# The last block's output stores: one transfer for each batch's 64 rows in place of one for two batches

## Chip, cores and metric

The kernel runs on one core of one Trainium2 chip. The metric is the device time of one execution in microseconds. Before the change it is 1684.03 us, the median of three runs (1682.93 to 1684.46).

## What is computed

A linear attention without softmax, normalized by its root mean square, then two feed-forward layers over the 4608 tokens (8 batches of 576):

```python
kv  = einsum('bhsd,bhse->bhde', k, v)          # q, k, v: (8, 8, 576, 64)
o   = einsum('bhsd,bhde->bhse', q, kv)
o   = o / sqrt(mean(o * o, -1) + 1e-6) * g_norm
x   = o.transpose(0, 2, 1, 3).reshape(4608, 512)
r   = maximum(x @ w_in1, 0)                    # w_in1: (512, 2048)
x   = (s * r * r + b) @ w_out1                 # w_out1: (2048, 512)
h   = x @ w_in2
out = (h / (1 + exp(-h))) @ w_out2             # out: (4608, 512)
```

## The kernel before

Every matmul operand is split into a rounded high part and the rest, and a product is three matmuls of 128 x 512 (`mm3`, lines 182 to 185). Tokens are taken in nine blocks of 512 columns (`NB`, `T`). Blocks 0 to 7 are the first 512 tokens of each batch. The ninth, called the last block here, gathers the 64 tokens that each of the eight batches has left (`REM` = 64, and 8 x 64 = 512).

Layer 1 takes the nine blocks one after the other (`unit`, lines 596 to 707) and writes its result to a scratch tensor in DRAM. Layer 2 takes blocks 0 to 7 in four pairs, by a scheme with seven products in place of eight (`hidden` and `outputs`, lines 820 to 954), and the last block by `unit` again, mixed with the last pair. Both kinds end in a tile with tokens on the 128 partitions and 512 output features in each row.

The order of the work is set by a planner (`Plan`, lines 16 to 116). Each operation has a key, the engines it may run on with a cost on each, and what it needs; the planner plays this through and issues the instructions in the order that comes out. All ordinary transfers are issued by SyncE (SP) through the helper `dma` in line 200, so all of them stand in the profile as L200.

What matters here runs at the very end. `block_out` (lines 709 to 736) takes a finished accumulator `a_t[d]` of the last block: `out_y` copies it to a part of the tile `x_t` (line 723, helper line 195; ScalarE does all four of them here), and `store` sends it to `out` (lines 731 and 732). There are four such accumulators, d = 0 to 3, one for each 128 of the block's 512 tokens, so that partitions 0 to 63 hold the last tokens of batch 2d and partitions 64 to 127 those of batch 2d + 1. In the tensor `out` the 64 rows of one batch lie in one piece, and those of the next batch lie 576 rows further on. `n = P // REM` is 2.

Between the second and the third of these four stores, the last pair's outputs are finished: VectorE adds the last products to a tile `y` (`total`, line 940), and SyncE stores it, 128 rows in one piece (line 953). Five such stores stand between them. The planner costs a store of `block_out` at 0.48 us on SyncE and 0.73 us of transfer (line 736).

Of the kernel before, what the change touches and what calls it, by code (L numbers as in the profile page):

```python
# [15 lines left out]
class Plan:  # L16
# [19 lines left out]
    def add(self, engines, key, fn, needs=(), makes=(), takes=(), gives=(), move=None, opens=(), until=None):  # L36
        self.ops.append((key, len(self.ops), engines, fn, needs, makes, takes, gives, move, opens, until))
        for b in gives:
            self.users[b] = self.users.get(b, 0) + 1
# [80 lines left out]
def kernel(  # L120
# [22 lines left out]
    B, H, S, D = q.shape  # L143
    NT, DM = out.shape
    DFF = w_in1.shape[1]
    P = 128
# [4 lines left out]
    T = NCH * P  # L151
    REM = S - T
# [40 lines left out]
    def copy(e, dst, src):  # L193
        if e == "ACT":
            nc.scalar.copy(dst, src)
        else:
            eng[e].tensor_copy(dst, src)

    def dma(dst, src):
        nc.sync.dma_start(out=dst, in_=src)  # L200
# [167 lines left out]
    def new_x(t):  # L368
        x_t[t] = xp.tile([P, KD, T], F32, tag="x32", name="x32")
# [339 lines left out]
    def block_out(layer, t, d, key, acc):  # L709
        lb = layer * NB + t  # L710
        st = {}
        yb = ("y", (lb, d))

        final = lb == 2 * NB - 1

        def out_y(e):
            if not final:
                st["y"] = tp.tile([P, T], F32, tag="y", name="y", bufs=2)
            else:
                if d == 0:  # L720
                    new_x(lb + 1)
                st["y"] = x_t[lb + 1][:, d]
            copy(e, st["y"], a_t[d])

        def store(e):
            if layer == 0:
                dma(y1[t, :, d], st["y"])
            elif t < NB - 1:
                dma(out[t * S + d * P:t * S + (d + 1) * P, :], st["y"])
            else:  # L730
                n = P // REM
                dma(out.rearrange("(b s) e -> b s e", s=S)[n * d:n * (d + 1), T:, :], st["y"])

        add({ACT: 0.52, DVE: 0.6}, key, out_y, needs=[("mm2", lb * KF + KF - 1, d)], makes=[("yc", lb, d)],
            takes=[("x32", lb + 1)] * (d == 0) if final else [yb], gives=[acc])
        add({"SP": 0.48}, key + 0.1, store, needs=[("yc", lb, d)], makes=[("y", lb, d)], gives=[] if final else [yb], move=0.73)
# [354 lines left out]
```

## Time and profile before

| | |
|---|---|
| median of three runs | 1684.03 us (1682.93 to 1684.46) |
| time of the profiled execution | 1683.55 us |
| its span | 1681.2 us |
| TensorE busy with matmuls | 1642.5 us, 98% of the span |
| VectorE, ScalarE, GpSimd busy | 51%, 39%, 34% |
| transfers | 236.28 MB, 141 GB/s in the mean |
| mean granted TensorE clock | 0.991 |

The span goes from the first instruction of the profiled execution to its last one; its own time is 2.35 us longer. Times in the views are counted from the start of the span. A share of busy DMA engines is that of all 16 together, so that one engine that works all the time is 0.0625. "To landing" is the time from the start of a transfer's issue to its completion, and the time in a row of an issue is how long SyncE was held by it. `out_dram<-x` are the four stores of the last block, `out_dram<-y` those of the pairs.

### The profile page before, as it was taken

To read this page: it belongs to the slowest core of one execution; us is meant where nothing else is said; L and a number is where in the kernel's file an instruction comes from. 1 tells how busy PE (TensorE), PEld (TensorE's weight loads), DVE (VectorE), ACT (ScalarE), POOL (GpSimd) and SP (SyncE) were. 2 spreads that over 40 slices of the span, in tenths; PEclk is the share of its full clock that TensorE was granted. 3 is DMA by queue.
4 is the path that set the end of the run, shared out by engine and by line. 5 is a ranking of instruction groups with operands and counts; after the bars stand their busy time and mean duration, and the time that the engine had idled before them with its cause. 6 is when DMAs were issued, how large, how long until landed. Compare 5 with 4: busy or idle time off the path is not lost.

```text
span 1681.2 us, 21306 instructions
## 1 busy us (share of the span) xinstructions
PE 1642.5 (98%) x7744; PEld 1334.1 (79%) x7744; DVE 865.4 (51%) x1313; ACT 658.5 (39%) x1198; POOL 565.3 (34%) x481
## 2 busy tenths in 40 slices
PE   8889999999999999999999999999999999999995
PEld 6667888888888888888887888888888888888884
DVE  6998666675656666534342244634463445344211
ACT  5666444444444444432333322432343234323221
POOL 4665343333434344210341223622362235223100
PEclk9989999999999999999999999999999999999998
DMA  9554445444444544210134444644464447444552
GB/s 218 173 157 125 134 127 158 139 147 126 138 143 129 168 122 150 99 63 1 51 116 128 126 145 140 229 156 143 142 232 148 139 138 237 138 140 141 183 156 81
DMA packets 226911, 236.28 MB, mean 141 GB/s; under 512 B 99832, under 2 KB 181752, under 8 KB 226680
## 3 DMA queue, kind: packets, MB, share of 16 engines
q1 hardware_dynamic: 226680, 234.94, 45.4%
q8 instruction: 61, 1.00, 0.3%
q14 instruction: 42, 0.34, 0.1%
q0 software_dynamic: 128, 0.00, 0.0%
HBM read 181.41 MB, written 53.48 MB: 140 GB/s over the span
## 4 chain that ended last, share of the span: by engine, by line
PE 91%; DVE 3%; DMA 1%; ACT 1%; issue 1%; SPq 1%; POOL 0%; DVEq 0%; ACTq 0%; POOLq 0%
PE hp L836 18%; PE h L184 8%; PE h L185 8%; PE h L183 8%; PE acc L183 8%; PE acc L184 7%; PE acc L185 7%; PE acc L931 7%; PE acc L932 7%; PE acc L930 7%; PE kv_ps L433 1%; PE acc L687 1%; PE acc L686 1%; PE acc L685 1%; DVE raw L263 1%
## 5 line engine op out<-in xcount | busy, mean ns | idle before, releaser
L836 PE MATMUL hp<-xo,win 128*128 128x512 f32 x1344 | 344.0, 390 | 0.8 <-DVE tmp L861 0.8
L191 POOL TENSOR_TENSOR g<-tmp,g 128x512 fp32r<-128x512 f32 x123 | 159.3, 1296 | 425.0 <-ACT g L188 223.5
L836 PEld LDWEIGHTS hp<-xo,win 128*128 128x128 f32 x1344 | 252.0, 188 | 57.6 <-DVE tmp L861 2.2
L940 DVE TENSOR_TENSOR y<-acc,y 128x512 f32<-128x512 f32 x224 | 154.3, 690 | 275.1 <-PE acc L932 273.0
L183 PE MATMUL acc<-gh,wo 128*128 128x512 f32 x576 | 234.4, 407 | 2.9 <-ACT gh L188 2.9
L184 PE MATMUL acc<-gl,wo 128*128 128x512 f32 x576 | 226.9, 394 | 5.8 <-DVE gl L191 2.8
L629 ACT ACTIVATE g<-h 128x512 f32<-128x512 f32 x160 | 95.5, 597 | 346.8 <-PE h L185 337.6
L184 PE MATMUL h<-xl,wi 128*128 128x512 f32 x576 | 226.8, 394 | 1.7 <-DVE xl L191 1.6
L183 PE MATMUL h<-xh,wi 128*128 128x512 f32 x576 | 226.5, 393 | 0.1
L185 PE MATMUL h<-xh,wi 128*128 128x512 f32 x576 | 226.1, 393 | 0.3 <-DVE wi L191 0.3
L185 PE MATMUL acc<-gh,wo 128*128 128x512 f32 x576 | 226.1, 392 | 0.0
L637 DVE SCALAR_TENSOR_TENSOR g<-g,vecs 128x512 f32<-128x512 f32 x128 | 104.0, 813 | 197.1 <-ACT g L629 197.0
L932 PE MATMUL acc<-wout,g 128*128 128x512 f32 x512 | 201.7, 394 | 0.0
L931 PE MATMUL acc<-wout,g 128*128 128x512 f32 x512 | 201.7, 394 | 0.0
L930 PE MATMUL acc<-wout,g 128*128 128x512 f32 x512 | 201.3, 393 | 0.0
L861 DVE TENSOR_TENSOR tmp<-hp,tmp 128x512 f32<-128x512 f32 x160 | 110.4, 691 | 99.3 <-PE hp L836 93.9
L665 DVE SCALAR_TENSOR_TENSOR gl<-g,vecs,gh 128x512 fp32r<-128x512 f32 x128 | 112.4, 878 | 49.3 <-ACT gh L659 48.1
L282 POOL TENSOR_TENSOR dw<-raw 128x256 uint32<-128x256 uint32 (+1 forms) x100 | 88.8, 890 | 137.3 <-DVE raw L268 87.3
L184 PEld LDWEIGHTS acc<-gl,wo 128*128 128x128 f32 x576 | 108.9, 189 | 28.1 <-DVE gl L191 4.4
L191 POOL TENSOR_TENSOR spill<-dw,spill 128x512 fp32r<-128x512 f32 x53 | 71.5, 1350 | 176.5 <-ACT spill L188 171.2
L184 PEld LDWEIGHTS h<-xl,wi 128*128 128x128 f32 x576 | 109.0, 189 | 27.2 <-DVE xl L191 3.7
L183 PEld LDWEIGHTS acc<-gh,wo 128*128 128x128 f32 x576 | 109.0, 189 | 26.4 <-ACT gh L188 4.2
(123 smaller groups left out, 2303.1 us busy)
## 6 DMA issues: line engine op xcount, KB each, us to landing
win<-wi SPq DMA_DIRECT2D x96, 512.0 KB, 4.5
wout<-wo SPq DMA_DIRECT2D x160, 256.0 KB, 4.1
wi<-spill SPq DMA_DIRECT2D x32, 512.0 KB, 2.6
wo<-spill SPq DMA_DIRECT2D x32, 512.0 KB, 2.9
win<-wi SPq DMA_DIRECT2D x64, 256.0 KB, 3.2
raw<-in_moe_w_out_dram SPq DMA_DIRECT2D x38, 256.0 KB, 3.0
y<-y SPq DMA_DIRECT2D x36, 256.0 KB, 2.6
raw<-in_moe_w_in_dram SPq DMA_DIRECT2D x34, 256.0 KB, 2.8
```

Source lines behind the costliest of these rows:

```text
L183: nc.tensor.matmul(ps, wh, xh, start=first, stop=False)
L184: nc.tensor.matmul(ps, wh, xl, start=False, stop=False)
L185: nc.tensor.matmul(ps, wl, xh, start=False, stop=last)
L191: eng[e].tensor_tensor(lo, src, f32(hi), op=ALU.subtract)
L637: nc.vector.scalar_tensor_tensor(out=g_t[u], in0=g_t[u], scalar=s_t, in1=g_t[u], op0=ALU.mult, op1=ALU.mult)
L665: nc.vector.scalar_tensor_tensor(out=st["g"][1], in0=g_t[u], scalar=b_t, in1=f32(st["g"][0]), op0=ALU.add, op1=ALU.subtract)
L836: nc.tensor.matmul(ps, w[:, wn, f_], x_[:, xn], start=first and n == 0, stop=kk == KH - 1 and n == 2, skip_group_check=True)
L861: nc.vector.tensor_tensor(t, bank[me, a], tmp[b_, me], op=ALU.add)
L930: nc.tensor.matmul(ps, g[:, 0, dd], w[:, 0], start=f == 0, stop=False)
L931: nc.tensor.matmul(ps, g[:, 0, dd], w[:, 1], start=False, stop=False)
L932: nc.tensor.matmul(ps, g[:, 1, dd], w[:, 0], start=False, stop=f == 1)
L940: nc.vector.tensor_tensor(y2[tp, tt], st["ps"], y2[tp, tt], op=ALU.add)
```

## The change

In the last block's branch of `store`, a loop over the two batches takes the place of the one transfer. Each transfer reads 64 partitions of the tile and writes 64 whole rows of `out`, which lie in one piece. Bytes and destinations are the same; four transfers of 256 KB become eight of 128 KB.

```diff
             elif t < NB - 1:
                 dma(out[t * S + d * P:t * S + (d + 1) * P, :], st["y"])
             else:
-                n = P // REM
-                dma(out.rearrange("(b s) e -> b s e", s=S)[n * d:n * (d + 1), T:, :], st["y"])
+
+                for i in range(P // REM):
+                    r = (P // REM * d + i) * S + T
+                    dma(out[r:r + REM, :], st["y"][i * REM:(i + 1) * REM])
```

The planner's costs for the operation are as before. On SyncE's queue, this is what stands at the end of the program before the change: the last load of weights, two stores of the last block (`x`, in the form 2 x 64 x 512), the five stores of the last pair (`y`), and the other two of the last block. Names in square brackets are what an instruction waits for; `DMAHW0` to `DMAHW7` are the eight semaphores that transfers take in turn, and a wait on one of them is for the transfer that had it before.

```order
L200 DMA wout<-wo_7_98 128x2x256
L200 DMA out_dram<-x_13837 2x64x512 [waits Activation_49] x2
L200 DMA out_dram<-y_12251 128x512 [waits DMAHW4_49,DVE_49]
L200 DMA out_dram<-y_12269 128x512 [waits DMAHW5_49,DVE_49]
L200 DMA out_dram<-y_12285 128x512 [waits DMAHW6_49,DVE_49]
L200 DMA out_dram<-y_12307 128x512 [waits DMAHW7_49,DVE_49]
L200 DMA out_dram<-y_12330 128x512 [waits DMAHW0_49,DVE_49]
L200 DMA out_dram<-x_13837 2x64x512 [waits DMAHW1_49,Activation_49]
L200 DMA out_dram<-x_13837 2x64x512 [waits DMAHW2_49,Activation_49]
```

The same place in the changed kernel, on SyncE, from the second store of the last block on (two more halves, those of the first store, stand just ahead):

```order
L200 DMA out_dram<-x_13837 64x512 [waits DMAHW4_49,Activation_49]
L200 DMA out_dram<-x_13837 64x512 [waits DMAHW5_49]
L200 DMA out_dram<-y_12251 128x512 [waits DMAHW6_49,DVE_49]
L200 DMA out_dram<-y_12269 128x512 [waits DMAHW7_49,DVE_49]
L200 DMA out_dram<-y_12285 128x512 [waits DMAHW0_49,DVE_49]
L200 DMA out_dram<-y_12307 128x512 [waits DMAHW1_49,DVE_49]
L200 DMA out_dram<-y_12330 128x512 [waits DMAHW2_49,DVE_49]
L200 DMA out_dram<-x_13837 64x512 [waits DMAHW3_49,Activation_49]
L200 DMA out_dram<-x_13837 64x512 [waits DMAHW4_49]
L200 DMA out_dram<-x_13837 64x512 [waits DMAHW5_49,Activation_49]
L200 DMA out_dram<-x_13837 64x512 [waits DMAHW6_49]
```

Each store of the last block has become two in the same place, and nothing has moved past another; the semaphore that a store takes has shifted by two for the y stores and by two to four for the last ones. The other engines have the same instructions in the same order.

## Rows read from the trace of the kernel before

**Rows 1.** Chain of waits, its last pieces: start us, us, what.

```profile
1662.01 0.24 PE acc L687
...
1662.28 0.59 ACT x L195
```

**Rows 2.** Busy time by stretches of the program's end, columns as in the first line.

```profile
core 0: us, PE busy (x) PEld busy (x) DVE busy (x) ACT busy (x) POOL busy (x), PEclk, DMA share, GB/s
1647.50:1654.50 7.00, 7.00 (x33) 5.77 (x32) 0.69 (x1) 2.37 (x4) 0.00 (x0) 1.00 0.00 0
1654.50:1658.00 3.50, 3.50 (x17) 2.84 (x16) 1.38 (x2) 0.04 (x1) 0.00 (x0) 1.00 0.13 33
1659.00:1662.00 3.00, 3.00 (x15) 2.30 (x13) 1.38 (x2) 0.40 (x1) 0.00 (x0) 1.00 0.94 287
1662.00:1664.00 2.00, 0.24 (x2) 0.00 (x0) 0.00 (x0) 0.77 (x2) 0.00 (x0) 1.00 0.85 244
1665.00:1680.00 15.00, 0.00 (x0) 0.00 (x0) 0.00 (x0) 0.00 (x0) 0.00 (x0) 0.51 0.13 49
1680.00:1681.20 1.20, 0.00 (x0) 0.00 (x0) 0.00 (x0) 0.00 (x0) 0.00 (x0) 0.50 0.00 0
```

**Rows 3.** SyncE's waits after 1663 us: total us, times, longest us.

```profile
SPq L1086 <- DMA out_dram<-x: 13.0, 2, 7.9
```

**Rows 4.** Timeline of SyncE's issues at the end: start us, us, what.

```profile
1653.26 0.65 SPq L200 DMA_DIRECT2D out_dram<-x  x1
...
1656.06 2.15 SPq L200 DMA_DIRECT2D out_dram<-y  x1
1658.31 0.45 SPq L200 DMA_DIRECT2D out_dram<-y  x1
1658.85 0.87 SPq L200 DMA_DIRECT2D out_dram<-y  x1
...
1661.64 0.33 SPq L200 DMA_DIRECT2D out_dram<-y  x1
1662.21 0.52 SPq L200 DMA_DIRECT2D out_dram<-x  x1
1662.89 4.05 SPq L200 DMA_DIRECT2D out_dram<-x  x1
```

**Rows 5.** Line 200, the y stores issued at 1656.06 and at 1661.64.

```profile
DMA to landing us min/median/max: 11.0/11.0/11.0
...
DMA to landing us min/median/max: 8.0/8.0/8.0
```

**Rows 6.** Transfers by line, 353 to 361 us: count, KB each, median us to landing.

```profile
y<-y SPq DMA_DIRECT2D x4, 256.0 KB, 2.5
```

**Rows 7.** Timeline of SyncE's issues, 350.9 to 354.4 us.

```profile
350.96 0.61 SPq L200 DMA_DIRECT2D rem<-in_k_dram  x1
351.61 0.60 SPq L200 DMA_DIRECT2D rem<-in_v_dram  x1
354.35 0.34 SPq L200 DMA_DIRECT2D y<-y  x1
```

**Rows 8.** Busy time by stretches, 353.0 to 353.6 us, columns as in rows 2.

```profile
353.00:353.20 0.20, 0.20 (x2) 0.17 (x1) 0.20 (x1) 0.00 (x0) 0.17 (x1) 1.00 0.25 58
353.20:353.40 0.20, 0.20 (x2) 0.16 (x2) 0.20 (x1) 0.00 (x0) 0.00 (x0) 1.00 0.33 73
353.40:353.60 0.20, 0.20 (x3) 0.15 (x2) 0.20 (x1) 0.00 (x0) 0.00 (x0) 1.00 0.37 80
```

**Rows 9.** Timeline of ScalarE, 1661 to 1663 us.

```profile
1661.60 1.26 ACT L195 COPY x<-acc 128x512 f32<-128x512 f32 x2 [7.06 <-PE acc L687]
```

**Rows 10.** SyncE's issues on the tile orem_d, 32 stores of 32 KB.

```profile
DMA to landing us min/median/max: 1.4/1.8/4.8
```

## Prediction

> **What bounds the kernel now.** I read the views from the end of the program backwards, since the edited line runs only there. The chain of waits comes first, and the reader should see where it stops: after the last matmul at 1662.01 us it takes one ScalarE copy at 1662.28 and ends at 1662.87, 18.3 us before the span is over at 1681.2 [rows 1]. The chain follows work on engines; what fills those 18.3 us has to be read from the transfers.
>
> The table by stretches shows it [rows 2]. From 1659 to 1662 the 16 DMA engines were busy for 0.94 of the time and moved 287 GB/s. From 1665 to 1680 they were busy for 0.13 and moved 49 GB/s, with every compute engine at zero. A share of 0.125 is two engines of sixteen at work all the time, 24.5 GB/s each. The same 0.13 stands in 1654.5 to 1658, when the first two stores of the last block were the only transfers in flight (nothing moved from 1647.5 to 1654.5). SyncE's waits agree: at the program's end it waits 13.0 us in two pieces for out_dram<-x, the stores of the last block [rows 3]; counted from the end of its last issue (1662.89 + 4.05 = 1666.94 us [rows 4]) that puts the last landing at 1679.94, and 1.2 us of closing steps follow.
>
> The reason lies in the form of the store. It is 2 batches x 64 rows x 512, and the share says that it is divided over its outermost count, two. Four such stores are 1.05 MB; the five stores in 128 x 512 form among them spread over all engines and give the same two engines another 2/16 of 1.31 MB, 0.16 MB. 1.21 MB at 49 GB/s is 24.7 us; from 1654.5 (first bytes) to 1679.9 are 25.4 us, so this queue on two engines, begun by the first of the four stores, explains the whole tail. Its traces are also in the other stores: the y store issued at 1656.06 held SyncE for 2.15 us [rows 4] and took 11.0 us to land, and that of 1661.64, when the other fourteen engines were nearly free, still 8.0 [rows 5]; the same 128 x 512 form took 2.5 us in the middle of the program [rows 6]. So **two DMA engines bound the last 18 us**; TensorE bounds the rest and is not touched.
>
> **The change, part by part.**
>
> *Spread.* Each 2 x 64 x 512 store becomes two of 64 x 512, whose outermost count is 64 rows on both sides. I take them to run on all sixteen engines, as the 128 x 512 stores do. The trace has one kind with 64 rows, the loads of the remainder rows: issued at 350.96 and 351.61, with no other issue until 354.35, they are what is left in flight at 353.0 to 353.6, at a share of 0.25 to 0.37, four to six engines [rows 7, 8]. So 64 rows spread over more than two. In a sentence by itself: the Trainium skill, page "DMA: Bandwidth & Descriptors", section "Why a DMA increments its semaphore by 16 and not by 1", gives as the number of engines the largest one up to 16 that divides the slowest sizes of both sides, which is two before (this trace agrees, 0.13) and sixteen after (no run shows that yet).
>
> *Four more issues on SyncE.* The two extra ones at 1653 to 1655 lie in its idle time. The other two lie on the path. The third store is released at 1662.21 as now, the fourth by the copy that ends at 1662.86 [rows 4, 9]. I price an issue by the unhindered 128 x 512 store, 0.33 us, plus 0.09 to the next instruction (0.45 from 1658.31 leaves 0.09 before 1658.85) [rows 4]: halves at 1662.21, 1662.63, 1663.05, and the last at 1663.47. Bounds: nothing extra (the last at 1662.89), or the 0.61 and 0.60 of the 64-row loads [rows 7], with which the last begins 0.84 us later, 1664.3.
>
> *Waits added.* The order gives the stores eight semaphores in turn, so that four more stores reach round sooner: the last y store waits for a half of the first store, and the last four for halves of the first two and for the first y store. All of those are issued by 1656.1 and would land some 3 us later, while the waits stand at 1661.6 and after. I cost them at nothing; that holds as long as the early halves land within 5 us. Nothing is queued behind the last of them but the end of the program.
>
> *The last landing.* From issue to landing a 256 KB store took 2.5 us [rows 6], a 32 KB one 1.8 in the median and at least 1.4 [rows 10]. For the last 128 KB half I take 2.4, close to the larger one, since three halves are just ahead of it: 1663.47 + 2.4 = 1665.9. The rate gives a check: first bytes come about 1.25 us after an issue (1653.26 to 1654.5), so those of the last y store at 1662.9; it and the last two blocks are 0.79 MB, at 287 GB/s 2.7 us, hence 1665.6. The lower bound is 1663.47 + 1.4 = 1664.9.
>
> *What stays.* TensorE, ScalarE, VectorE and GpSimd keep their order, and no instruction on them waits for these stores. The 1.2 us of closing steps stay.
>
> **The sum.** The end moves from 1681.2 to 1665.9 + 1.2 = 1667.1, a gain of 14.1 us. Against the profiled execution's own 1683.55 us that is 1669.45. The median of the runs shown, 1684.03, stands 0.48 above that execution, so for the median I forecast **1669.9 us**. With the lower landing it is 1.0 less, 1668.9. What bounds the end then is TensorE's last matmul, one copy, the last store and the closing steps.
>
> **A rule that speaks against it.** The rows show that one 2 x 64 x 512 store in two batches runs on two engines [rows 2]. The Trainium skill's page "DMA: Bandwidth & Descriptors", section "Rules for kernel authors", advises not to split a transfer into its two partition halves, because both halves use the same sixteen engines and go one after the other. By that rule alone two issues of 0.42 us would be added and nothing gained, 1684.9. The premise of sixteen engines isn't met by the store of this kernel, by the 0.13 of the row, so I give it only the weight of the third rival below.
>
> **The rivals.**
>
> 1. *Half the rate for half the partitions.* Each new store reads only rows 0 to 63 or 64 to 127 of its tile. If half the partitions yield half the rate, the last 0.52 MB go at 144 GB/s instead of 287: 3.65 us in place of 1.83, the end 1.8 us later, **1671.7**. For it: no row shows a large transfer from 64 partitions on many engines. Against: halves of both kinds follow each other and could overlap. The Trainium skill, page "SBUF — State Buffer", section "Door 1: The DMA port swizzle (why [64,N] ≈ [32,N])", says that 64 partitions reach eight of sixteen ports; no row here tests it. Chance 0.20.
>
> 2. *One engine (slower).* If the engines followed the number of batches in a store, one batch would have one engine: the same one for all eight halves. It would carry 1.05 MB plus 1/16 of 1.31 MB, 1.13 MB at 24.5 GB/s, 46.1 us from 1654.5, to 1700.6, plus 1.2: the span grows by 20.6, the median to **1704.6**. It decides for fewer than two engines; at two the time stands still. For it: two batches had exactly two. Against: the loads of 64 rows at a share of 0.25 to 0.37, where one engine is 0.06 [rows 8]. Chance 0.03.
>
> 3. *No change.* If the two engines come from something that stays (the tile, the output's rows), the same bytes drain in the same time, 1684.0, at most 0.9 more for two later issues. Against: the y stores go to the same output tensor at a share of 0.94 among others [rows 2]. Chance 0.02.
>
> **How the numbers follow.** My forecast has 0.75. Of the cases, forecast and half rate are faster: 0.95; no change 0.02; slower 0.03. A measurement of this kernel can tell about 0.2% from no change, 3.4 us, and both faster cases are well beyond it. The range takes in the lower landing (1668.9) less the 1.0 us or so by which the quickest run shown stands under the median, and above, half rate with the slow issues, 1671.7 + 0.8: **1667.9 to 1672.5**.
>
> **What would show it.** In the changed kernel's table by stretches no stretch at 0.13 is left in the tail; the share from 1655 to 1662 lies between 0.4 and 0.7, moves in bursts, and falls to zero by about 1666. The y store at 1656.06 no longer holds SyncE for 2 us, and all y stores land in about 2.5 to 3 us. SyncE's wait for out_dram<-x shrinks from 13.0 to about 2, and the span is near 1667. Half rate would show in the last halves: the share at 1663 to 1666 near 0.5 and a later end. I am wrong if a stretch of 0.06 or 0.13 remains, if the issues on SyncE are longer than 0.6 us each, or if one of the added waits stands before 1661.6 on a half that hasn't landed.

## Result, and the profile after

The changed kernel takes 1669.3 us in the median of four runs (1667.89 to 1669.53), the kernel before beside it 1683.62 (1682.93 to 1684.46): a ratio of 0.9913, with a 95% interval of 0.9896 to 0.993, or 14.3 us. The forecast was 1669.9, with a range of 1667.9 to 1672.5. The profiled execution took 1669.53 us with a span of 1667.3.

The stretches of the program's end, in the changed kernel, columns as in [rows 2]:

```profile
1654.50:1658.00 3.50, 3.50 (x17) 2.84 (x16) 1.38 (x2) 0.00 (x0) 0.00 (x0) 1.00 0.85 216
1655.00:1662.00 7.00, 7.00 (x31) 5.46 (x30) 3.46 (x5) 0.49 (x1) 0.00 (x0) 1.00 0.66 207
1664.00:1666.00 2.00, 0.00 (x0) 0.00 (x0) 0.00 (x0) 0.00 (x0) 0.00 (x0) 1.00 0.84 184
```

No stretch at 0.13 is left. Where two engines began to work off the first store alone at 33 GB/s [rows 2], 216 GB/s move now, and everything has landed by 1666.3.

SyncE's waits from 1650 us on, in the changed kernel (total us, times, longest us), answer to [rows 3]:

```profile
SPq L200 <- ACT x L195: 8.8, 2, 8.6
SPq L200 <- DVE y L942: 4.1, 5, 1.0
SPq L1088 <- DMA out_dram<-x: 1.5, 3, 0.6
```

The wait for the landings at the program's end fell from 13.0 to 1.5 us. There is no row in which L200, an issue, waits for a transfer: the semaphores' waits cost nothing. SyncE's issues, in the changed kernel, answer to [rows 4]:

```profile
1653.17 0.54 SPq L200 DMA_DIRECT2D out_dram<-x  x1
...
1655.97 0.36 SPq L200 DMA_DIRECT2D out_dram<-y  x1
...
1662.12 0.47 SPq L200 DMA_DIRECT2D out_dram<-x  x1
1662.64 0.59 SPq L200 DMA_DIRECT2D out_dram<-x  x1
1663.33 0.55 SPq L200 DMA_DIRECT2D out_dram<-x  x1
1663.92 0.59 SPq L200 DMA_DIRECT2D out_dram<-x  x1
```

No issue is held for 2 or 4 us any more. Of the ten stores issued from 1655 us on (the five y stores, the second store's second half and the last four halves), from issue to landing:

```profile
DMA to landing us min/median/max: 2.0/2.2/2.5
```

The first of the y stores takes 2.1 us and the last 2.0, where [rows 5] had 11.0 and 8.0; each of the last four halves takes 2.3 to 2.4, and the last landing is at 1666.3.

The last matmul of the changed kernel begins here, and is 0.39 us long:

```profile
1661.76 0.39 PE L687 MATMUL acc<-wout,gl 128*128 128x512 f32 x1
```

So it ends at 1662.15, and **the tail behind it**, from there to the end of the span, is 5.1 us (the span before rounding is 1667.25). Before it was 18.9 (1681.17 less 1662.24: the last matmul began at 1661.85). The difference, 13.8 us, is nearly the whole gain; TensorE's part did not change. The tail is the measure of choice for what follows, since the end of the last matmul itself varies: it is 1662.15 and 1663.21 us in two profiles of the changed kernel, and lies between 1661.8 and 1665.2 in the twelve profiles of this study. Work far ahead of these stores varies by more than a microsecond.

### The profile page after: what moved, and what is told of

Read it like the earlier page. It is cut to its first block, busy times and chain, and to the rows that moved or that the text cites. A ratio compares the mean times of both kernels' runs of the same rounds, so it can differ in the third digit from the quotient of the medians.

```text
span 1667.3 us, 21311 instructions
## 1 busy us (share of the span) xinstructions
PE 1641.2 (98%) x7744; PEld 1334.0 (80%) x7744; DVE 866.3 (52%) x1313; ACT 658.2 (39%) x1198; POOL 564.8 (34%) x481
## 4 chain that ended last, share of the span: by engine, by line
PE 91%; DVE 4%; DMA 1%; issue 1%; SPq 1%; ACT 1%; POOL 0%; DVEq 0%; ACTq 0%; POOLq 0%
PE hp L838 18%; PE h L184 8%; PE h L185 8%; PE h L183 8%; PE acc L183 8%; PE acc L184 7%; PE acc L185 7%; PE acc L933 7%; PE acc L934 7%; PE acc L932 7%; PE kv_ps L433 1%; DVE raw L263 1%; SPq L200 1%; PE acc L685 1%; PE acc L686 1%
```

## Experiments

The theory: the outermost count of a store's form sets how many DMA engines carry it, two before and sixteen now, and those two were a queue that began with the first store. The rivals: smaller transfers as such; the last stores alone; half the rate for half the partitions; one engine for one batch.

**More transfers without more engines.**

```diff
-                for i in range(P // REM):
-                    r = (P // REM * d + i) * S + T
-                    dma(out[r:r + REM, :], st["y"][i * REM:(i + 1) * REM])
+                n = P // REM
+                for c in range(2):
+                    cc = slice(c * DM // 2, (c + 1) * DM // 2)
+                    dma(out.rearrange("(b s) e -> b s e", s=S)[n * d:n * (d + 1), T:, cc], st["y"][:, cc])
```

> Each of the four stores is cut into two by columns, so that there are eight of 128 KB as in the change, but each still has two batches as its outermost count. My theory (the outermost count sets the engines): two engines carry the same 1.21 MB, the tail stays at a DMA share of 0.13 from 1665 us to the end, and the time is that of the kernel before, 1684, or up to 3 us more, since the pieces are half as long. Rival (smaller and more transfers are what helps): about 1669 to 1672.

Measured: 1684.62 us (1683.99 to 1686.1), a ratio of 1.0007 to the kernel before (0.9997 to 1.0018). A stretch of its end:

```profile
1668.00:1681.00 13.00, 0.00 (x0) 0.00 (x0) 0.00 (x0) 0.00 (x0) 0.00 (x0) 0.50 0.13 46
```

Eight transfers of 128 KB, as in the change, and the share stays at two of sixteen engines. The number and size of the transfers give nothing here, as long as the outermost count stays two.

**The split on the last two stores alone, and on the first two alone.** The loop stays, with the old transfer ahead of it for two of the four; in the second run the condition is `d >= 2`:

```diff
+                if d < 2:
+                    n = P // REM
+                    dma(out.rearrange("(b s) e -> b s e", s=S)[n * d:n * (d + 1), T:, :], st["y"])
+                    return
                 for i in range(P // REM):
```

> Only the third and the fourth store are split by batch, the first two stay as before. My theory (a queue on two engines): these two carry 0.52 MB of the first two stores and 2/16 of 1.84 MB, 0.75 MB at 49 GB/s, 15.4 us from 1654.5, so the last landing is at 1669.9, the span 1671 and the time 1673.2, 11 us under the kernel before. Rival (only the form of the last stores counts, the early ones are hidden behind matmuls): 1669.3, the full gain.

> Only the first and the second store are split by batch, the last two stay as before. My theory: the two engines begin with the third store, first bytes at 1663.4, and carry 0.52 MB at 49 GB/s, 10.7 us, so the last landing is at 1674.1, the span 1675 and the time 1677.4. Rival (the queue that the first store begins is what makes the tail): 1669 to 1671.

Measured: with the last two split 1674.62 us (1673.99 to 1675.4), a ratio of 0.9946 (0.993 to 0.9963); with the first two split 1679.96 (1677.65 to 1681.31), 0.9975 (0.9965 to 0.9984). Both rivals fall, as neither pair alone gives the full gain. Both medians lie above the theory's numbers, by 1.4 and 2.6 us.

In the first run, one issue waits for a transfer (SyncE's waits from 1663 us on):

```profile
SPq L200 <- DMA out_dram<-x: 2.8, 1, 2.8
```

By the rotation of the eight semaphores that is a half of the fourth store, issued only at 1666.13, when the second store, still on two engines, has landed. This is the added wait that the prediction priced at nothing under the condition that the early halves land early; here they don't. But it isn't shown to cost anything. The first half of the third store, issued at 1661.93 without such a wait, takes 7.7 us to land (1669.6), and the last half of all, issued at 1666.72, takes 3.9 (1670.6). Stretches of this run:

```profile
1655.00:1658.00 3.00, 3.00 (x15) 2.42 (x14) 1.53 (x3) 0.00 (x0) 0.00 (x0) 1.00 0.13 35
1667.00:1669.00 2.00, 0.00 (x0) 0.00 (x0) 0.00 (x0) 0.00 (x0) 0.00 (x0) 0.50 0.65 165
1669.40:1669.90 0.50, 0.00 (x0) 0.00 (x0) 0.00 (x0) 0.00 (x0) 0.00 (x0) 0.50 0.13 49
```

The fourth store's halves move mostly between 1667 and 1669; what comes last is two engines alone, at 0.13, which work off their queue. The profiled execution (1673.99) is 0.8 us over the theory's 1673.2, and the first row gives about that much: for 3.0 us the queue moved 35 GB/s where the theory took 49, which is 0.04 MB, 0.9 us at 49 GB/s. The median is another 0.6 us over this execution.

In the second run the tail is one long stretch on two engines, after an early part at full width:

```profile
1655.00:1658.00 3.00, 3.00 (x15) 2.42 (x14) 1.38 (x2) 0.00 (x0) 0.00 (x0) 1.00 0.93 239
1663.50:1667.00 3.50, 0.00 (x0) 0.00 (x0) 0.00 (x0) 0.00 (x0) 0.00 (x0) 0.63 0.12 31
1667.00:1675.00 8.00, 0.00 (x0) 0.00 (x0) 0.00 (x0) 0.00 (x0) 0.00 (x0) 0.50 0.13 51
```

Its profiled execution (1678.81 us, span 1676.6, last matmul over at 1662.49) has a tail of 14.1 us where 12.8 had been worked out. The second row gives the other 1.3 us: for 3.5 us the queue moved 31 GB/s in place of 49, which is 0.06 MB, 1.3 us at 49 GB/s. The kernel before has the same slow beginning (33 GB/s in [rows 2]); why two engines begin slowly is not shown. The median's further 1.2 us over this execution is within the spread of the runs.

**One engine.**

```diff
                 for i in range(P // REM):
                     r = (P // REM * d + i) * S + T
-                    dma(out[r:r + REM, :], st["y"][i * REM:(i + 1) * REM])
+                    for a, b2 in ((0, 61), (61, 64)):
+                        dma(out[r + a:r + b2, :], st["y"][i * REM + a:i * REM + b2])
```

> Each batch's 64 rows are stored as 61 and 3 rows; 61 has no divisor up to 16 but 1. My theory (the engines are the largest number up to 16 that divides the outermost count): all eight stores of 61 rows run on one and the same engine, 1.0 MB plus 1/16 of 1.31 MB, 1.08 MB at 24.5 GB/s, 44 us from 1654.5; a DMA share of 0.06 in the tail, the span about 1700 and the time 1702, slower than the kernel before. Rival (any store of one batch is spread over all engines): 1669 to 1674, a little more than the change for eight more issues.

Measured: 1702.6 us in both runs, a ratio of 1.0111 (1.0091 to 1.0131). Its stretches:

```profile
1655.00:1658.00 3.00, 3.00 (x15) 2.43 (x14) 1.38 (x2) 0.00 (x1) 0.00 (x0) 1.00 0.06 16
1676.00:1698.00 22.00, 0.00 (x0) 0.00 (x0) 0.00 (x0) 0.00 (x0) 0.00 (x0) 0.50 0.07 26
```

One engine of sixteen is 0.0625, and one engine at 26 GB/s carries the tail. Sixteen transfers that each hold one batch, in one piece of DRAM, are 33 us slower than eight of 64 rows. So it is the divisors of the outermost count that matter, not the number of batches nor contiguity. The Trainium skill's page "DMA: Bandwidth & Descriptors", section "Why a DMA increments its semaphore by 16 and not by 1", has the rule (the largest number up to 16 that divides the slowest sizes of both sides); counts of 2, 61 and 64 agree with it here, with shares of 0.13, 0.06 to 0.07, and 0.84 and more. No run reads the share of a count that the rule would put on more than two and fewer than sixteen engines.

**Half the partitions, and the price of an issue.** Two runs ask what spaces the last four halves.

```diff
-                    dma(out[r:r + REM, :], st["y"][i * REM:(i + 1) * REM])
+                    dma(out[r:r + REM, :], st["y"][P // 4:P // 4 + REM])
```

> Both stores of a pair read partitions 32 to 95 in place of 0 to 63 and 64 to 127; the rows written are the same, their contents are not the reference's for the last block. Bytes, rows and number of transfers are those of the change. If the half of the partitions that a store reads sets its rate, the rate while only such stores are in flight (205 GB/s at a share of 0.94 in the changed kernel) goes up to that of the y stores (262 GB/s at 0.69, so some 350 at a share of 0.94) or the share falls to about 0.55 at the same rate, and the last landing comes 0.3 us earlier; if moreover the 0.59 us of an issue is held by the transfers ahead, issues shrink to 0.35 and the end comes about 1 us earlier. Rival (the rate is that of 64-row stores whatever the partitions): nothing changes.

Measured: 1670.13 us (1669.83 to 1670.42). The row of the changed kernel was 1664 to 1666 above, a share of 0.84 at 184 GB/s. This run, with only such stores in flight:

```profile
1664.50:1666.40 1.90, 0.00 (x0) 0.00 (x0) 0.00 (x0) 0.00 (x0) 0.00 (x0) 1.00 0.56 207
```

Divided by the engines that were busy, that is 184 / (16 x 0.84) = 13.7 GB/s for each before, and 207 / (16 x 0.56) = 23.1 now. Partitions 32 to 95 give a busy engine 1.7 times what partitions 0 to 63 or 64 to 127 give it. The mechanism of the prediction's first rival is there. The Trainium skill's page "SBUF — State Buffer", section "Door 1: The DMA port swizzle (why [64,N] ≈ [32,N])", says that the halves 0 to 63 and 64 to 127 each reach eight of the sixteen ports; the 13.7 against 23.1 GB/s of this run agree with it, though no row shows a port. But the time moved little: the last half lands 2.1 us after its issue in place of 2.4, and the last issue is as long as before:

```profile
1664.67 0.58 SPq L200 DMA_DIRECT2D out_dram<-x  x1
```

0.58 us with engines that are half free: the issue is not held by the transfers ahead. Nor was the very first half of the changed kernel, 0.54 us at 1653.17, ahead of which nothing was in flight. The issue spaces the halves at some 0.6 us, and a half at the lower rate (128 KB at 16 x 13.7 GB/s) takes 0.6 us too. The slower rate hides behind the issues, all but the last one's 0.3 us.

```diff
-                for i in range(P // REM):
-                    r = (P // REM * d + i) * S + T
-                    dma(out[r:r + REM, :], st["y"][i * REM:(i + 1) * REM])
+                for i in range(P // 32):
+                    r = (P // REM * d + i // 2) * S + T + i % 2 * 32
+                    dma(out[r:r + 32, :], st["y"][i * 32:(i + 1) * 32])
```

> Each store of the last block is four of 32 rows, sixteen in all. They should still run on all engines, as 32 is divisible by 16. Theory A (an issue's time follows the transfer behind it, 0.59 us for 64 rows because 128 KB takes that long): 0.3 us each, the last issue begins near 1664.8 and the end is within 0.3 us of the change, 1669 to 1670. Theory B (an issue has a price of its own, some 0.5 to 0.6 us whatever the rows): the last of eight begins at 1662.1 + 7 x 0.64 = 1666.6, lands at 1668.8, span 1669.8, 2.5 us over the change, about 1671.8.

Measured: 1669.91 us (1669.72 to 1670.1), span 1667.6, last matmul over at 1661.76, a tail of 5.8 us. One of the last eight issues:

```profile
1664.92 0.43 SPq L200 DMA_DIRECT2D out_dram<-x  x1
```

Neither theory had it: 32 rows take 0.33 to 0.43 us, not 0.3 and not 0.6. Twice the issues cost 0.7 us in the tail: the last one begins 3.2 us after the last matmul's end in place of 1.8, and a landing of 1.7 us in place of 2.4 gives half of it back. So theory A's time (1669 to 1670) came out, though its 0.3 us for an issue did not.

**Two queues.**

```diff
-                    dma(out[r:r + REM, :], st["y"][i * REM:(i + 1) * REM])
+                    (nc.sync, nc.scalar)[i].dma_start(out=out[r:r + REM, :], in_=st["y"][i * REM:(i + 1) * REM])
```

> ScalarE issues the second half of each store, SyncE the first. If SyncE's issues in a row are what spaces the last four halves, the last issue begins at about 1663.4 in place of 1663.9 and the tail behind the last matmul shrinks by about 0.5 us, less what ScalarE's own issue of the third store delays its fourth copy by. If the rate of the halves spaces them, the landing takes longer instead and the tail stays at 5.1 us.

Measured: 1671.39 us (1671.22 to 1671.57); last matmul over at 1664.27, span 1669.1, a tail of 4.8 us. ScalarE's timeline, and the landing of its halves (count, KB each, median us), show why only 0.3 us came of it:

```profile
1664.25 0.50 ACTq L734 DMA_DIRECT2D out_dram<-x  x1
1664.79 0.58 ACT L195 COPY x<-acc 128x512 f32<-128x512 f32 x1 [0.58 <-PE acc L687]
1665.41 0.50 ACTq L734 DMA_DIRECT2D out_dram<-x  x1
out_dram<-x ACTq DMA_DIRECT2D x2, 128.0 KB, 2.7
```

The fourth copy begins 0.52 us after the last matmul's end, behind ScalarE's own issue. Where SyncE issues everything, the two copies stand together, 1.26 us for both [rows 9]. Even so the last issue begins 1.14 us after the last matmul's end (1665.41 less 1664.27), where the change has 1.77 (1663.92 less 1662.15): 0.6 us earlier. A half issued by ScalarE then takes 2.7 us to land in place of 2.4, and 0.3 us of the 0.6 are gone; why it takes longer is not shown. The median lies above the change's because the last matmul ends 2.1 us later, which comes from far ahead of the stores: by 1500 us this execution has 7026 matmuls, that of the changed kernel 7035, and a matmul takes 0.23 us here.

**Another last store.** What is left of the tail is a copy, four issues one after the other and a landing. If a 128-row store came last, only one issue would stand there.

```diff
-            add({"PE": 0.648}, u + LAG2 + d * 0.02, mm2(d),
+            add({"PE": 0.648}, u + LAG2 + d * 0.02 - 18 * (layer == 1 and m == KF - 1), mm2(d),
...
-                block_out(layer, t, d, u + LAG2 + d * 0.02, acc)
+                block_out(layer, t, d, u + LAG2 + d * 0.02 - 18 * (layer == 1), acc)
```

> The change, with the last block's closing matmuls given keys 18 lower, so that its third and fourth accumulator are finished among the pair's outputs and a y store of 128 rows comes last. The tail behind the last matmul is then 0.7 us on VectorE, 2.0 us from one issue to landing and 1.0 us of closing steps, 3.8 us in place of 5.1: 1.3 us under the change, about 1668.0. Rival (the closing steps wait for something else): 1669.3.

Measured: 1669.74 us (1668.3 to 1670.14), a ratio of 0.9905 (0.9888 to 0.9922). The last matmul:

```profile
1663.91 0.40 PE L934 MATMUL acc<-wout,g 128*128 128x512 f32 x1
```

The matmul ends at 1664.31 and the span at 1668.0: a tail of 3.7 us against 3.8 worked out, 1.4 less than with the change. It doesn't show in the medians, as the last matmul of this execution ends 2.2 us later than that of the changed kernel. It has 7026 matmuls by 1500 us in place of 7035, nine times 0.23 us, and up to there the order of the matmuls is the same in both. Both were run once more, side by side.

> The changed kernel itself, beside the next run on the same chip: about 14 us under the kernel before, and 5.1 us from the end of the last matmul to the end of the span.

> The kernel with the last block's closing matmuls ahead of the pair's last outputs, beside the changed kernel on the same chip: 3.7 us from the end of the last matmul to the end of the span, in place of 5.1, and a median 1.4 us lower. If the stretch up to the last matmul varies by more than that from run to run, the tail shows the gain in both profiles and the medians may not.

Measured: the change 1670.49 us (1669.13 to 1671.73), a ratio of 0.992 (0.9906 to 0.9934); the other order 1669.99 (1668.94 to 1671.05), 0.9916 (0.9903 to 0.993). The tails are 1668.3 - 1663.21 = 5.1 and 1668.9 - 1665.22 = 3.7 us, the same as before. The gain in the tail is shown twice; the medians differ by 0.5 us, well inside the spread, so that a gain of this order over the change in the total time is not shown. Here too the last matmul ends 2.0 us later than beside it, with 7022 matmuls by 1500 us against 7030; whether that is chance in both pairs stays open.

All tails together, from the end of the last matmul to the end of the span:

| kernel | tail, us |
|---|---|
| before | 18.9 |
| eight column pieces, on two engines | 1682.4 - 1662.46 = 19.9 |
| first two stores split | 14.1 |
| last two stores split | 1671.7 - 1661.96 = 9.7 |
| 61 and 3 rows | 1700.4 - 1662.71 = 37.7 |
| the change | 5.1 |
| quarters of 32 rows | 5.8 |
| partitions 32 to 95 | 1667.7 - 1662.87 = 4.8 |
| second half from ScalarE | 4.8 |
| a pair's store last | 3.7 |

## Why the prediction was right

*What bounds the end.* Right: two engines, read from a DMA share of 0.13. The stores in columns (same number of transfers, same two engines, no gain) and those of 61 rows (one engine, 1702.6 us) settle it. The queue begins with the first store and the last two add to it, as the two half-splits show.

*Spread.* Right. 64 rows run on all engines: shares of 0.84 to 0.93 while such stores are in flight.

*Four more issues.* The term was sized too low. I took 0.33 us from the 128-row store; the 64-row store takes 0.47 to 0.59, near the upper bound that the loads of 64 rows gave. The last issue began at 1663.92, against 1663.47 forecast, although everything ahead of it was 0.09 us early: half a microsecond too little.

*Waits added.* Right, nothing: the early halves land 2.3 to 2.5 us after their issue. With the last two stores alone split, the condition named there fails and such a wait stands there, 2.8 us; it lies beside the queue of the two engines, which ends later, so that what it would cost by itself is not shown.

*The last landing.* 2.4 us forecast, 2.4 measured, but not for the reason given, so that this agreement is in part luck. The rate was taken to be that of the full stores, and from these partitions a busy engine gave 13.7 GB/s in place of 23.1.

*The closing steps.* The end is 1667.3, with the last landing at 1663.92 + 2.4 = 1666.3: 1.0 us in place of 1.2. Together: 0.5 later by the issues, 0.2 earlier by the closing steps, and 1667.3 for 1667.1. That the span is met so closely owes something to these two errors, which go against each other. Of the median's 0.6 us (1669.9 forecast, 1669.3 measured) most is no term of the kernel: the forecast put the median 0.48 above the profiled execution, as before the change, and it came out 0.23 below it. For the profiled execution itself 1669.45 stood against 1669.53.

*The rivals.* Half the rate for half the partitions is a fact and not a rival: a busy engine gave 0.6 of the rate. Its price was wrong, 0.3 us in place of 1.8, since the issues space the halves anyway. "One engine" was priced about right (1704.6 forecast, 1702.6 measured with 61 rows), but it isn't the number of batches that leads to it. The Trainium skill's page "DMA: Bandwidth & Descriptors", section "Rules for kernel authors", advises against splitting a transfer into its two partition halves; that did not hold here, since the undivided transfer did not have the sixteen engines that the rule supposes. Of the signs named, the share from 1655 to 1662 came out as said (0.4 to 0.7 forecast, 0.66 measured). Two were off: the y stores land in 2.0 to 2.1 us in place of 2.5 to 3, and the sign for half the rate, a share near 0.5 at the end, would have missed it, as the rate fell while the engines' share stayed at 0.84.

## What to carry to other kernels

A DMA share that stands still at a small multiple of 1/16 is a count of engines: look for a transfer whose outermost count has no large divisor up to 16, and give it a count that 16 divides, even at the price of more transfers. Many rows alone are not enough: 64 ran on all engines here, and 61 on one. A queue like that can lie hidden under matmuls and come out only at the end, and the chain of waits may not show it; compare its last piece with the end of the span. When the change is in a tail, measure from the last instruction that the change doesn't touch; the rest of the program may vary by more than the tail moves.

## What was not expected of the hardware

An issue's time does not follow its bytes or rows in any simple way: 128 rows take 0.33 to 0.36 us on SyncE, 64 rows 0.47 to 0.60, 32 rows 0.33 to 0.43, and 61 rows, which go to one engine, 0.32 where nothing is in the way. That the 64 rows' issue is not held by transfers in flight is shown by the changed kernel's first half (0.54 us with nothing ahead of it) and by the run on partitions 32 to 95 (0.58 us with the engines half free); what it is stays open.
